# Spreading both halves of a key tile in one VectorE operation, loading a weight in two parts, and a new instruction order, in a four-layer attention kernel

## The chip, the cores and the metric

The kernel runs on one core of a Trainium2 chip, as one launch. The metric is the device time in microseconds; the median of three runs of the kernel before is 464.93 us (463.89 to 466.02). The profile is of one execution, with a span of 462.5 us from the first to the last instruction.

The engines are called as the profile calls them: PE is TensorE (matrix multiplication; PEld is its weight load), DVE is VectorE, ACT is ScalarE, POOL is GpSimd and SP is SyncE, which here issues only transfers. Both SP and ACT issue transfers ("SPq" and "ACTq" in the profile).

## The reference

Four layers are applied to x, 2048 rows of 512 numbers, with residual additions. Layers 1 and 3 are sliding-window attention with weights A; layers 2 and 4 are linear attention with weights B. There are 32 heads of 16 numbers each.

```python
def _A_ref(x, wqkv, wo):            # window of 256 keys
    qkv = (x @ wqkv) ...            # q, k, v by head
    scores = einsum("bhqd,bhkd->bhqk", q, k) * (Dh ** -0.5)
    mask = (i - j >= 0) & (i - j < W)
    p = softmax(where(mask, scores, -1e9))
    return einsum("bhqk,bhkd->bhqd", p, v) ... @ wo

def _B_ref(x, wqkv, wo):            # linear attention
    phi = lambda t: where(t > 0, t + 1, exp(t)) + 1e-6
    pq, pk = phi(q), phi(k)
    kv = einsum("bhsd,bhse->bhde", pk, v);  z = sum of pk over s
    o = einsum("bhqd,bhde->bhqe", pq, kv) / (pq . z + 1e-6)
    return o ... @ wo

x = x + _A_ref(layernorm(x), A_wqkv, A_wo)
x = x + _B_ref(layernorm(x), B_wqkv, B_wo)
x = x + _A_ref(layernorm(x), A_wqkv, A_wo)
x = x + _B_ref(layernorm(x), B_wqkv, B_wo)
```

## The kernel before

The rows are treated in four blocks I of 512. Every piece of work is recorded as an operation with the engines that may do it, and a fixed list, `ORDER`, says in which order the 2582 operations are emitted and on which engine each runs (18H is operation 18, a transfer; P is PE, A is ACT, V is DVE, G is POOL, S is SP). A small model of the engines, the planner, walks through this list. It does not choose the order; it chooses which bank of PSUM (the accumulator memory of PE, eight banks) each operation takes, and puts filler matmuls (`fill`) where it expects PE to stand idle.

```python
def is_warm(t):                      # does the planner expect PE at full clock at time t?
    k = int(t / self.WIN)
    for w in range(max(warm, default=-1) + 1, k + 1):
        warm[w] = mac.get(w - 1, 0) >= self.FULL
    return warm[k]
...
if start - free["PE"] > self.GAP:    # an expected gap of PE: fill it with matmuls of the identity
    ...
    fill = (b[0], m) if m else fill
...
def fill(k, n):
    for _ in range(n):
        nc.tensor.matmul(psb[:, k, :], lhsT=identb[:], rhs=..., start=True, stop=True)      # line 491
```

The keys. A projection writes 128 rows (8 heads) by 512 keys to one bank of PSUM. The scores need every key twice, once with the rows of the other head of a pair set to zero. So the result is multiplied by `eo`, a pair of 0/1 columns, and each key becomes two neighbouring columns. Five buffers of 256 keys each (`NH = 5`) are used in rotation; `half(8*I)` and `half(8*I+4)` are the two of block I: 0 and 1, 2 and 3, 4 and 0, 1 and 2.

```python
NH, NPT = 5, 5
kbd = [fp.tile([P, NCT, 4, 64, 2], BF, name=f"kbd{k}") for k in range(NH)]

def k_unit(key, I, t):
    o, s, ps = proj(... wA columns of k, tile t ..., reads=[B("wA", 1, min(t, 1))], ...)   # 4 matmuls, line 569
    for hf in range(2):
        r = half(8 * I + 4 * hf)
        def fe(e, hf=hf, r=r):
            if e == "ACT":
                for h in range(2):
                    nc.scalar.mul(kbd[r][:, t, :, :, h], ps()[:, hf*256:(hf+1)*256]..., eo[:, h:h+1])   # line 777
                return
            nc.vector.tensor_tensor(kbd[r][:, t, :, :, :]..., ps()[:, hf*256:(hf+1)*256]...,
                                    eo[:]..., op=ALU.mult)                                              # line 779
        pl.op({"DVE": .68, "ACT": .9}, fe, reads=[B("eo")], deps=[o], writes=[B("k", r, t)], use=[s])
```

The rest of an attention block: `scores` multiplies queries with these keys (line 822), ACT takes the exponential (line 840), DVE or POOL zeroes what is outside the window (lines 868 and 873), and `pv_group` multiplies with the values (line 901). The values get from a staging tile to their place by transfers on SP (`vbd<-vst`, line 798). The normalised rows reach PE transposed, as `xnT`, by a transposing transfer on SP (line 579) or by PE itself (line 588); layernorm writes them to `xn` (line 701 on DVE), and a buffer of `xn` is free again once its transpose has read it.

The weights. Five parts of `wA` and the first rows of x are loaded at once. The other loads are issued by ACT where the order puts them; the time given first is the earliest at which the planner lets one start:

```python
for b, t, c, fn in ((b_x[8:NT], 15.0, 3.0, lambda e: load_x(nc.scalar, 8, NT - 8)),
                    ([B("woA")], 25.0, 1.5, lambda e: nc.scalar.dma_start(woA[:], wcols(A_wo, 0))),
                    ([B("wB")], 40.0, 4.5, lambda e: nc.scalar.dma_start(wB[:], wcols(B_wqkv, 0, 3))),
                    ([B("woB")], 70.0, 1.5, ...)):
    o = pl.op({"ACT": .5}, fn, after=t)
    pl.op({"HBM": c + 2.0}, lambda e: None, deps=[o], writes=b)
```

`wB` is the weight of the linear layers, read by `bk_unit` and `bv_unit` (columns 512 to 1535, keys and values) and by `bq_units` (columns 0 to 511, queries).

Of the kernel before, what the change touches and what calls it, by code (L numbers as in the profile page):

```python
# [9 lines left out]
ALU = mybir.AluOpType  # L10
F32 = mybir.dt.float32
BF = mybir.dt.bfloat16
# [138 lines left out]
class Planner:  # L151
# [25 lines left out]
    def run(self):  # L177
# [7 lines left out]
        def is_warm(t):  # L185
            k = int(t / self.WIN)
            for w in range(max(warm, default=-1) + 1, k + 1):
                warm[w] = mac.get(w - 1, 0) >= self.FULL
            return warm[k]
# [50 lines left out]
18H 17H 36V 6G 19H 20H 12A 41V 46V 37G 38V 51A 14A 23H 2G 42G 15A 13A 21H 3G 47G 10V 22H 24H 43V 39P 40V 25H 44P  # L240
52V 48V 45V 75P 76V 49P 53P 54V 77S 78P 50V 26H 65P 55P 79V 60P 62A 63P 16V 57V 56V 67A 0G 58P 80S 314V 59V 66V
64V 61A 27A 329V 73P 87P 88A 81P 4G 9G 1G 91P 84P 28H 82A 83S 5G 70P 315G 316V 319V 330G 324V 89G 96P 72V 71V
92A 7G 320G 101P 74A 85A 325G 95G 102A 321V 90G 68P 69V 317P 97A 107P 322P 86S 104G 94G 98G 106G 103G 108A 109G
115P 105G 99G 116A 331V 318V 354P 93G 332P 119P 323V 617V 618G 8G 100G 120A 110G 124P 117G 355V 326V 357P 125A
333V 629V 625V 621V 123G 129P 356S 327P 111P 112P 113P 128G 630G 130A 131G 358A 133V 328V 122V 135P 143P 114V
136A 121V 127G 619V 126G 134V 360P 144A 132G 147P 137G 118G 138G 631V 361V 359S 337P 620S 148A 916V 152P 139P
140P 153A 157P 928V 622G 141P 626G 158A 142V 149G 146G 160G 162G 155V 156G 363P 150G 161G 338A 364V 163P 171P
627V 623V 154V 164A 166G 165G 334P 347P 632S 362S 917G 159G 151G 175P 348V 172A 145V 336V 342P 343V 173G 920V
335V 180P 176A 185P 653P 181A 167P 168P 169P 174V 654V 186A 29A 921G 624S 628S 191P 199P 177G 183G 179V 918V
365S 192A 646P 170V 636P 647V 187V 190V 929G 184G 182G 203P 188G 189G 178V 200A 656P 208P 204A 194G 31A 213P  # L250
657V 193V 637V 201G 195P 641P 214A 196P 217V 206G 197P 209A 215V 930V 219P 227P 220A 642V 352P 216V 228A 198V
212G 211G 205G 218G 221G 924V 202G 207G 233P 210V 651P 652V 234A 366P 222G 232G 223P 224P 225P 371P 237V 655S
229G 230G 658S 235V 236G 238G 367A 372A 353V 231G 375P 376A 925G 239P 662P 373G 931S 379G 380P 226V 240V 659P
919S 374G 370G 663V 926V 381A 660V 369G 386P 339P 340V 341V 378V 387A 922V 377G 390P 391A 384V 344P 346V 398P
242S 345V 385G 633P 382G 635V 399A 248S 403P 349P 383G 251S 368G 389G 407P 245S 388G 393V 400V 634V 394P 392G
401V 923S 927S 404A 408A 402G 412P 395P 396P 418P 351V 413A 419A 416V 414V 935P 422P 423A 415V 405V 664S 417G
409G 410G 406V 350V 430P 397V 431A 936V 638P 421G 435P 436A 411V 420V 424V 643P 439P 426P 645V 440A 425G 444P
427P 445A 428P 450P 451A 644V 454P 639V 648P 446G 449G 437G 640V 438V 432V 452G 434V 455A 448G 661S 429V 433V
462P 940P 467P 453V 463A 443G 457G 468A 442G 447G 456V 932P 471P 941V 441G 458P 649V 241V 472A 459P 476P 477A
465G 460P 482P 650V 933V 934V 937P 483A 469V 464V 486P 243P 494P 487A 495A 474V 475V 461V 470V 244V 466G 479G  # L260
480G 945P 499P 500A 484V 481G 473V 488V 478G 489V 485G 490P 497V 939V 946V 938V 503P 504A 491P 508P 492P 514P
254V 505G 509A 510G 512G 493V 507G 515A 511V 249P 518P 519A 246P 32H 250V 516V 498G 526P 502G 527A 33A 517G 255G
247V 506G 513G 520G 532G 252P 521V 942P 536P 665P 501V 253V 496V 522P 530G 535G 523P 524P 944V 528G 537A 534G
533G 541V 540V 666A 531G 538G 529V 539V 670P 542P 674P 671A 675A 525V 543V 262V 551S 545S 548S 554S 952P 679P
680A 673V 685P 258V 943V 678V 953V 955P 672V 263G 677G 668G 686A 667G 256G 681V 956V 689P 688G 687G 690A 683G
684G 682G 257S 950P 669V 697P 698A 546P 702P 552P 692V 676V 547V 703A 706P 691G 693P 707A 711P 694P 557V 553V
565V 712A 699V 264G 695P 717P 270P 705G 259G 718A 951V 721P 729P 555P 271A 696V 549P 957S 722A 713G 558G 709V
720G 715V 704V 559V 266V 700V 730A 714G 710G 716G 719G 734P 735A 556V 701G 708G 723G 738P 724V 550V 569V 725P
743P 265S 954S 739A 260V 744A 731G 261S 267G 566G 726P 727P 749P 750A 732V 742G 958P 747G 570G 753P 754A 728V
272V 959V 544V 274P 761P 766P 762A 275V 741V 755V 746V 273V 767A 961P 571G 751V 756G 737G 745G 740G 733G 276P  # L270
770P 775P 962V 768V 752G 736G 284P 748V 757P 758P 759P 277A 776A 769V 771A 561V 278V 777V 781P 285A 780G 782A
279V 773V 760V 778V 785P 786A 560S 280P 793P 794A 764V 763G 774G 288P 798P 799A 572S 286V 287V 765G 562G 779G
567V 947P 802P 784G 772G 803A 783V 289V 789P 807P 563G 788G 787V 790P 808A 810G 949V 801V 805G 795V 568S 564S
948V 281V 791P 811G 804G 960S 813P 814A 815G 282P 605P 606A 268V 792V 797V 817P 818A 796V 806G 825P 601P 602A
283V 816V 826A 819G 812V 607V 963S 800G 613P 614A 809G 835P 608V 832G 827G 820G 833G 836A 603V 604V 609P 830V
831V 615V 964P 610A 965A 829G 828V 821P 822P 823P 969P 834V 616V 839G 840G 837G 838V 824V 841P 842V 970A 269S
290P 291A 973P 974A 978P 979A 844S 967G 971G 847S 850S 611V 981G 294P 612V 573P 295V 984P 985A 292V 293V 968V
966G 980G 845P 988P 989A 848P 982V 983G 996P 997A 846V 976V 972G 1001P 849V 991G 1002A 574A 853S 990G 975V 860V
986G 987G 977G 851P 852V 577P 1005P 1006A 992P 861G 1010P 1011A 864V 578V 856V 575V 576V 993P 994P 1016P 1017A
998G 296P 857G 1020P 995V 1015V 1021A 1012G 1013V 854P 1014V 1028P 1029A 297V 579P 580A 1033P 1034A 1008G 587P  # L280
1007G 1018G 1037P 1038A 1009G 1019V 11V 1004V 999G 1000G 1003G 1023V 855V 1022V 1031V 858G 1024P 1025P 1026P
1042P 1043A 1048P 1049A 1044G 1030G 865G 581V 582V 1027V 868V 1039G 862G 583P 1052P 588A 1053A 1041V 584V 591P
1060P 1061A 592V 593P 585P 859S 1032G 35S 589V 590V 586V 1065P 1066A 863S 1035V 1046V 1040V 1047G 594A 1045G
1050G 1055V 597P 876P 1069P 1070A 598V 1036G 843V 1051G 1074P 1075A 1056P 1064G 1054G 866G 1057P 877V 1077G
1068V 867S 1058P 1067G 1080P 1081A 595V 1072V 882P 596V 1084P 1085A 599P 1079V 883V 1092P 1063G 1073G 1059V 872P
1076V 600V 1078G 890P 1093A 1071G 1097P 891V 873A 1098A 298P 299A 1101P 1102A 874V 1106P 878P 1082G 875V 1107A
1083V 1062V 869G 1087G 1086V 300V 1095V 1088P 1089P 879A 1090P 1112P 1113A 870G 871S 1110G 1100G 1104G 1099V
1116P 1117A 301V 886P 1091V 1105G 880V 1111G 1103G 302P 881V 1096V 884P 1109G 1108V 1115V 887A 303A 1124P 1134P
1114G 1094G 885V 1119G 1118G 888V 304V 889V 305V 1120P 1121P 1122P 1135A 1123V 1125A 34H 1133V 1132V 1131V 892P
1139G 1136G 893A 894V 1129V 1138G 895V 896P 1137G 1128G 1127G 306P 1126G 897A 1130G 1140P 898P 1141V 1143P 899V  # L290
1142V 307A 1144A 1151P 308G 1152V 1147P 1148A 1155P 1145P 1149P 309V 900P 1153P 1146V 1156A 1157P 1150V 1237V
1159A 1160A 1161G 1164V 1154V 1165A 310P 901A 1158V 1169A 1162P 1163V 1174A 1238P 1239V 904P 902V 1166G 1170G
311A 1167P 903V 1179P 312V 1171G 313V 1175G 1183P 1168A 905A 1172P 1189P 906V 1173A 1176G 907V 1185P 1193P 1180A
1184A 1186A 1181V 1190V 1182V 1177P 1178V 1194A 1187V 1188V 1195G 1197P 908P 1207P 1198V 1196V 1208A 1191P 1199P
1200A 1203P 1209V 1192V 1210V 1201V 1202V 909A 1215P 1204A 1216A 1217V 1218V 1211P 1205P 1206V 1223V 912P 913A
1225V 1219P 1240P 1241P 1224G 910V 1220A 1212A 914V 915V 1242A 1226G 911V 1213V 1227P 1214V 1243A 1221G 1228A
1222V 1244V 1851P 1538P 1539V 1233P 1536P 1235P 1537V 1234A 1231P 1236A 1247P 1248V 1232A 1229P 1852P 30H 1245P
1230A 1540P 1246V 1853A 1541V 1546P 1249P 1250V 1854A 1251P 1252V 1253P 1254V 1544P 1548A 1545V 1855V 1255P
1542P 1549G 1257A 1258G 1262A 1259G 1267A 1263A 1256V 1547V 1264G 1260P 1268A 1261A 1543V 1856P 1272A 1265P
# [76 lines left out]
def build(ctx, tc, A_x, A_wqkv, A_wo, B_x, B_wqkv, B_wo, out, force_safe=False):  # L376
# [95 lines left out]
    def fast_network(ctx_f):  # L472
# [52 lines left out]
        def B(*key):  # L525
            return bufs.setdefault(key, Buf())
        def half(m):
            return (m // 4) % NH
# [913 lines left out]
```

## Time and profile before

| | busy us | share of the span | instructions |
|---|---|---|---|
| PE | 436.0 | 94% | 6035 |
| DVE | 367.7 | 79% | 969 |
| ACT | 379.1 | 82% | 442 |
| POOL | 259.6 | 56% | 737 |

The page lists, for each engine, the busy time; then the span in 40 slices with one digit of busy share for each; then the chain of work that ended last. The groups of instructions follow, by line and shape: how many, their busy time together, the mean of one, and what ended the idle time of the engine before them. In a timeline, the first column is the start and the second the duration of a merged run of instructions; square brackets hold the idle time of that engine before it and what ended it. Matmuls overlap one another, so that the listed duration of one is longer than the distance from one to the next.

### The profile page before, as it was taken

The page shows a single profiled execution, that of the slowest core. Times are in us where ns is not written, and L with a number is a line of the kernel's source. Part 1 is how long each engine was busy: PE and PEld are TensorE (multiplying, and loading weights), DVE is VectorE, ACT ScalarE, POOL GpSimd, SP SyncE. Part 2 cuts the span into 40 slices and gives each one's busy share as a digit, 9 for nine tenths or more (in the row PEclk, how much of TensorE's full clock was granted, in tenths as well). Part 3 has the DMA queues.
Part 4 walks back from the last instruction along what each step waited for, and adds up shares of the span by engine and source line. Part 5 has one row for each costly group of instructions (what it writes and reads, how often), then busy time and mean ns, then how long its engine had stood idle before and what let it go on. Part 6 is the DMA issues. An engine that isn't in the chain of part 4 may idle for free.

```text
span 462.5 us, 15167 instructions
## 1 busy us (share of the span) xinstructions
PE 436.0 (94%) x6035; PEld 227.6 (49%) x6103; DVE 367.7 (79%) x969; ACT 379.1 (82%) x442; POOL 259.6 (56%) x737
## 2 busy tenths in 40 slices
PE   6997999999999999999999998999999989999893
PEld 2454454555555556543445454555455545464331
DVE  5996687878887987878887888888887786777883
ACT  7798599989999999655888888989999989967630
POOL 5298354367755575532325586855685549455432
PEclk8999899999999999999999999999999999999998
DMA  7424631023222010000021124111322122100014
GB/s 227 122 45 119 171 81 28 1 72 71 38 48 60 13 26 15 2 1 0 4 46 26 28 44 73 40 36 26 71 53 45 23 28 27 23 2 1 1 45 144
DMA packets 53806, 22.29 MB, mean 48 GB/s; under 512 B 38368, under 2 KB 53216, under 8 KB 53728
## 3 DMA queue, kind: packets, MB, share of 16 engines
q1 hardware_dynamic: 49760, 16.80, 17.2%
q10 hardware_dynamic: 3968, 4.46, 3.0%
q8 instruction: 49, 0.80, 0.7%
q14 instruction: 29, 0.24, 0.2%
HBM read 6.29 MB, written 2.10 MB: 18 GB/s over the span
## 4 chain that ended last, share of the span: by engine, by line
PE 75%; ACT 8%; issue 5%; DVE 5%; DMA 4%; POOL 2%; SPq 1%; ACTq 0%; DVEq 0%; POOLq 0%
PE psb L569 40%; PE psb L901 16%; PE psb L822 14%; ACT pt L840 7%; DMA wA<-in_A_wqkv_dram 2%; PE psb L1117 1%; PE psb L588 1%; DMA vbd<-vst 1%; DMA oT<-o_sb 1%; SPq L798 1%; POOL pqT L978 1%; PE psb L491 1%; PE psb L1091 1%; POOL pt L873 1%; DVE pqT L981 1%
## 5 line engine op out<-in xcount | busy, mean ns | idle before, releaser
L840 ACT ACTIVATE pt<-psb 128x1536 bf16<-128x1536 f32 (+2 forms) x246 | 284.1, 1215 | 30.8 <-PE psb L822 19.8
L873 POOL TENSOR_SCALAR_AFFINE_SELECT pt<-pt 128x192 bf16<-128x192 bf16 (+2 forms) x535 | 158.3, 330 | 112.0 <-ACT pt L840 107.9
L822 PE MATMUL psb<-qT,kbd 32*128 32x320 bf16 (+4 forms) x1440 | 94.0, 254 | 4.0 <-ACT pt L840 2.8
L901 PEld LDWEIGHTS <-pt 128*128 128x128 bf16 x2880 | 77.9, 96 | 13.6 <-issue 9.8
L901 PE MATMUL psb<-vbd,pt 128*128 128x34 bf16 x2880 | 83.7, 178 | 0.2 <-DVE xres L755 0.2
L868 DVE TENSOR_TENSOR pt<-pt,tri 128x128 bf16<-128x128 bf16 (+4 forms) x262 | 63.5, 275 | 12.1 <-ACT pt L840 11.8
L822 PEld LDWEIGHTS <-kbd 32*128 32x128 bf16 x1440 | 40.2, 92 | 66.3 <-issue 59.9
L569 PE MATMUL psb<-xnT,wA 128*128 128x512 bf16 x241 | 63.8, 387 | 3.6 <-issue 2.8
L569 PE MATMUL psb<-wB,xnT 128*128 128x512 bf16 x235 | 61.6, 380 | 1.6 <-DVE pqT L978 0.4
L569 PEld LDWEIGHTS <-xnT 128*128 128x128 bf16 x384 | 32.6, 98 | 42.5 <-issue 12.8
L779 DVE TENSOR_TENSOR kbd<-psb,eo 128x512 bf16<-128x512 f32 x58 | 37.8, 679 | 2.9 <-PE psb L569 2.6
L569 PEld LDWEIGHTS <-wA 128*128 128x128 bf16 x256 | 21.9, 99 | 30.1 <-issue 10.4
L569 PE MATMUL psb<-wA,xnT 128*128 128x512 bf16 x116 | 33.2, 392 | 2.7 <-DMA wA<-in_A_wqkv_dram 1.9
L569 PE MATMUL psb<-woA,oT 128*128 128x512 bf16 x120 | 31.5, 381 | 3.1 <-DMA oT<-o_sb 1.3
L569 PE MATMUL psb<-xnT,wB 128*128 128x512 bf16 x121 | 31.5, 380 | 0.9 <-DVE vflags L968 0.5
L569 PE MATMUL psb<-wkv,pqT 128*128 128x512 bf16 x123 | 29.6, 380 | 0.3
L690 DVE BATCH_NORM_STATS2 ln_st<-xres 128x6 f32<-128x512 f32 (+1 forms) x39 | 26.5, 680 | 1.7 <-DMA xres<-in_A_x_dram 1.6
L916 DVE TENSOR_TENSOR o_sb<-psb,rall 128x384 bf16<-128x384 f32 (+1 forms) x48 | 24.6, 513 | 1.7
L975 ACT ACTIVATE pqT<-psb 128x512 bf16<-128x512 f32 x32 | 18.9, 599 | 8.2 <-PE psb L569 6.4
L556 DVE CAST qT<-psb 128x512 bf16<-128x512 f32 x29 | 19.8, 685 | 6.9 <-PE psb L569 6.3
L624 POOL TENSOR_TENSOR ln_rs<-ln_rs,mhalf 128x1 f32<-128x1 f32 x39 | 21.9, 562 | 3.2
L981 DVE SCALAR_TENSOR_TENSOR pqT<-psb,pqT 128x512 bf16<-128x512 f32 x32 | 21.8, 687 | 1.6 <-POOL pqT L978 1.0
(122 smaller groups left out, 485.9 us busy)
## 6 DMA issues: line engine op xcount, KB each, us to landing
vbd<-vst SPq DMA_DIRECT2D x128, 34.0 KB, 1.9
out_dram<-ost SPq DMA_DIRECT2D x16, 128.0 KB, 1.8
wB<-in_B_wqkv_dram ACTq DMA_DIRECT2D x1, 1536.0 KB, 7.9
xres<-in_A_x_dram ACTq DMA_DIRECT2D x1, 1024.0 KB, 5.5
xnT<-xn SPq DMA_TRANSPOSE x40, 2.5
wA<-in_A_wqkv_dram SPq DMA_DIRECT2D x1, 512.0 KB, 7.1
xres<-in_A_x_dram SPq DMA_DIRECT2D x1, 512.0 KB, 8.1
woA<-in_A_wo_dram ACTq DMA_DIRECT2D x1, 512.0 KB, 5.7
```

Source lines behind the costliest of these rows:

```text
L556: (nc.scalar.copy if e == "ACT" else nc.vector.tensor_copy)(dst(), src())
L569: nc.tensor.matmul(t["t"][:], lhsT=lhs(c), rhs=rhs(c), start=(c == 0), stop=(c == NCT - 1))
L624: nc.gpsimd.tensor_tensor(out, out, mhalf[:, 0:1], op=ALU.pow)
L690: nc.vector.bn_stats(t["st"][:], x())
L779: nc.vector.tensor_tensor(kbd[r][:, t, :, :, :].rearrange("p m k h -> p (m k) h"), ps()[:, hf * 256:(hf + 1) * 256].unsqueeze(2).to_broadc ...
L822: nc.tensor.matmul(A[:, x, at[x]:at[x] + w, :], lhsT=kbd[half(m)][32 * rg:32 * rg + 32, tt, m % 4, :, :], rhs=qT[I % 2][32 * rg:32 * rg + ...
L840: nc.scalar.activation(body[:, x:y, 0:pos[x], :], t["A"][:, x:y, 0:pos[x], :], ACT.Exp, scale=0.25)
L868: nc.vector.tensor_tensor(v, v, mt, op=ALU.mult)
L873: nc.gpsimd.affine_select(out=v, in_=v, compare_op=ALU.is_ge, fill=0.0, base=1 if kind == 0 else -2, pattern=[[0, n], [2 * sg, 64]], chann ...
L901: nc.tensor.matmul(t["O"][:, u, g, :, :], lhsT=PT[:, s0:s0 + 2, :], rhs=vbd[half(m)][:, m % 4, :, grp[g], :], start=(n == 0), stop=(n == l ...
L916: nc.vector.tensor_tensor(o_sb[:, u0:u0 + nu, h0 * DH:(h0 + 2 * ng) * DH].rearrange("p u (h e) -> p u h e", e=DH), Ov[:, :, :, 0:DH], r.to ...
L981: nc.vector.scalar_tensor_tensor(out=dst(), in0=ps()[:], scalar=1.0 + 1e-6, in1=dst(), op0=ALU.add, op1=ALU.max)
```

## The change

It has five parts. The first takes the two halves of a key tile together: the five buffers become one tile, so that two neighbours lie side by side, and where the two of a block are neighbours (blocks 0, 1 and 3; not block 2, which has 4 and 0), one VectorE operation spreads all 512 keys. In these blocks ACT can no longer do it.

```diff
-        kbd = [fp.tile([P, NCT, 4, 64, 2], BF, name=f"kbd{k}") for k in range(NH)]
+        kall = fp.tile([P, NH, NCT, 4, 64, 2], BF, name="kall")
+        kbd = [kall[:, k] for k in range(NH)]
...
+            r0 = half(8 * I)
+            if r0 + 1 < NH:
+                def fe(e):
+                    nc.vector.tensor_tensor(kall[:, r0:r0 + 2, t, :, :, :].rearrange("p r m k h -> p r (m k) h"),
+                                            ps().rearrange("p (r c) -> p r c", r=2).unsqueeze(3).to_broadcast([P, 2, 256, 2]),
+                                            eo[:].unsqueeze(1).unsqueeze(1).to_broadcast([P, 2, 256, 2]), op=ALU.mult)
+                pl.op({"DVE": 1.2}, fe, reads=[B("eo")], deps=[o], writes=[B("k", r0 + hf, t) for hf in range(2)], use=[s])
+                return
             for hf in range(2):
```

The second loads `wB` in two parts, keys and values first, and lets these loads come earlier in the planner's time; the readers name the part that they need:

```diff
-                            reads=[B("wB"), B("xq", i)], ...          # bk_unit, bv_unit
+                            reads=[B("wB", 1), B("xq", i)], ...
-                                    reads=[B("wB")] + ...             # bq_units
+                                    reads=[B("wB", 0)] + ...
-                            ([B("woA")], 25.0, 1.5, lambda e: nc.scalar.dma_start(woA[:], wcols(A_wo, 0))),
-                            ([B("wB")], 40.0, 4.5, lambda e: nc.scalar.dma_start(wB[:], wcols(B_wqkv, 0, 3))),
+                            ([B("woA")], 19.0, 1.5, lambda e: nc.scalar.dma_start(woA[:], wcols(A_wo, 0))),
+                            ([B("wB", 1)], 22.0, 3.0, lambda e: nc.scalar.dma_start(wB[:, :, D:3 * D], wcols(B_wqkv, 1, 2))),
+                            ([B("wB", 0)], 27.0, 1.5, lambda e: nc.scalar.dma_start(wB[:, :, 0:D], wcols(B_wqkv, 0))),
```

The third moves the times at which the planner expects the first transfers to land. The fourth makes it assume a full PE clock from 25 us on:

```diff
+            if t > 25.0:
+                return True
...
-        ... ([B("wA", 2)], 8.0), ([B("wA", 1, 1)], 10.0), ([B("wA", 0, 1)], 9.5), (b_x[4:8], 12.0)]
+        ... ([B("wA", 2)], 9.5), ([B("wA", 1, 1)], 11.0), ([B("wA", 0, 1)], 10.5), (b_x[4:8], 12.5)]
```

The fifth is a new `ORDER` for all operations, 2560 of them now (cut):

```diff
-18H 17H 36V 6G 19H 20H 12A 41V 46V 37G 38V 51A 14A 23H 2G 42G 15A 13A 21H 3G 47G 10V 22H 24H 43V 39P 40V 25H 44P
-... (131 more lines)
+18H 17H 19H 0G 20H 38V 48V 39G 49G 15A 43V 44G 2G 53A 10V 40V 50V 23H 45V 54V 46P 6G 25H 24H 21H 1G 47V 41P 26H
+... (130 more lines)
```

What it is for: fewer operations on the engine that empties PSUM, each of which has a fixed cost; weights that are there before they are needed; and an order that fits the changed costs.

## The prediction

> **What bounds the kernel now.** I read four views: the page (busy shares, slices, chain), the groups by shape, the timeline of two stretches, and the busy time in stretches of 10 us. The page first.
>
> ```profile
> PE 436.0 (94%) x6035; PEld 227.6 (49%) x6103; DVE 367.7 (79%) x969; ACT 379.1 (82%) x442; POOL 259.6 (56%) x737
> PE   6997999999999999999999998999999989999893
> ACT  7798599989999999655888888989999989967630
> PEclk8999899999999999999999999999999999999998
> PE 75%; ACT 8%; issue 5%; DVE 5%; DMA 4%; POOL 2%; SPq 1%; ACTq 0%; DVEq 0%; POOLq 0%
> ```
>
> PE is the bound nearly everywhere: 75% of the chain that ended last, 9 tenths in most slices. In the attention blocks ACT is close behind it; from 50 to 180 us the stretches show PE busy 9.2 to 9.95 of 10 us and ACT 8.3 to 9.7. DVE, which the change relieves, is at 79% and has 5% of the chain. So time can come only from what makes PE idle or slow: 26 us of the span have no matmul at all. In the stretches these are 3.7 us before 10 us, 7.6 us after the last matmul, 2.8 us in 40 to 50, and about 1.4 us each in 280 to 290 and 370 to 380. The slice with PE 7 and the ACT 5 in the same place is the largest inner one. The timeline there:
>
> ```profile
> 38.76 2.52 SPq L579 DMA_TRANSPOSE xnT<-xn  x2
> ...
> 40.78 0.38 ACTq L1136 DMA_DIRECT2D woA<-in_A_wo_dram  x1
> ...
> 46.16 3.28 PE L569 MATMUL psb<-xnT,wA 128*128 128x512 bf16 x7 [2.67 <-issue]
> 46.16 0.41 DVE L701 TENSOR_SCALAR xn<-xres,ln_mv,ln_rs 128x512 bf16<-128x512 bf16 x1 [2.78 <-POOL pt L873]
> ```
>
> PE stops for 2.67 us and DVE for 2.78 us and both start again at 46.16. The names of the releasers mislead: in the built program both wait for the transposes xnT<-xn issued at 38.76. Their median is 2.5 us to landing; these took about 6, because the load of woA (0.5 MB, 5.7 us to landing by the page) was issued at 40.78 in the middle of them. Then PE is slow: 7 matmuls take 3.28 us, where a long run elsewhere in the chain has 33 in 7.23 us, 0.22 each. ACT next starts an exponential only at 50.02, after 4.37 us idle. The stop cost 2.67 + (3.28 - 7 x 0.22 = 1.7) = 4.4 us.
>
> The start, from the same view:
>
> ```profile
> 8.06 5.80 ACT L550 COPY vbd<-zero 128x2176 bf16<-128x2176 bf16 x3
> 9.28 1.86 PE L569 MATMUL psb<-wA,xnT 128*128 128x512 bf16 x4 [1.90 <-DMA wA<-in_A_wqkv_dram]
> ...
> 14.23 1.87 DVE L548 MEMSET vbd<- 128x2176 bf16 x1 [0.40 <-DVE vst L556]
> ...
> 16.02 1.22 DVE L779 TENSOR_TENSOR kbd<-psb,eo 128x512 bf16<-128x512 f32 x2
> 16.14 2.10 ACT L777 ACTIVATE kbd<-psb,eo 128x256 bf16<-128x256 f32 x5
> ...
> 19.13 1.45 ACT L840 ACTIVATE pt<-psb 128x1536 bf16<-128x1536 f32 x1 [0.89 <-PE psb L822]
> ```
>
> The first weights land at 9.28 and the first exponential starts at 19.13. Between them DVE clears a buffer for 1.87 us before it spreads keys, and ACT spends 15.73 to 18.24 on six key halves' columns.
>
> **What the Trainium skill says.** "VectorE: DVE Perf Modes", section "The TRN2 errata", says that an operation pays a fixed extra latency whatever its size, so that larger operations pay it less often. The groups agree for one operation alone:
>
> ```profile
> L779 DVE TENSOR_TENSOR kbd<-psb,eo 128x512 bf16<-128x512 f32 x58 | 37.8, 679 | 2.9 <-PE psb L569 2.6
> L1121 DVE TENSOR_TENSOR pqT<-pqT,psb 128x1024 bf16<-128x1024 bf16 x16 | 19.1, 1216 | 3.4 <-PE psb L1117 3.1
> L777 ACT ACTIVATE kbd<-psb,eo 128x256 bf16<-128x256 f32 x12 | 5.0, 549 | 1.9 <-PE psb L569 1.9
> ```
>
> Twice 679 is 1358, one of double size is 1216. But two back to back take 1.22 us together in the start above: the next begins before the first has ended, and the saving is gone. "DMA: Bandwidth & Descriptors", section "Issuing engines are not separate DMA queues", says that transfers issued by different engines run on the same 16 DMA engines; the slowed transposes beside woA agree. "TensorE: Matmul & The Clock Gate", Part 1, says that an idle PE falls to half clock and needs some 3.4 us of work to come back; the seven slow matmuls (0.43 us apart in the same timeline) agree. "Perfetto Trace Analysis", section "Identifying the Most-Contended Engine", warns that matmul busy time doesn't tell the headroom of PE; I therefore count gaps and pace, not the 94%.
>
> **The change part by part.**
>
> 1. Merged spreading. Of 64 halves, 58 were on DVE and 6 on ACT (12 instructions). Now 48 halves are 24 merged operations and 16 stay single on DVE, none on ACT. DVE: 24 x 1.216 - 42 x 0.679 = 29.2 - 28.5 = +0.7 us. ACT: -12 x 0.549 = -6.6 us. So the part named first saves VectorE nothing in total; it takes work off ACT. On the path it is worth little, because kbd stands in front of PE for almost no time (no wait of PE names it); half of ACT's 12 instructions are at the start, half at 190 to 238 us, where ACT is less loaded (5 to 8 us of 10). I count 0 here and leave the start to part 3.
> 2. The new order moves other operations between engines. Counting instructions of each shape in both built orders and multiplying by the mean of the groups: ACT -5.6 us in all (three value evacuations come to it, at 0.60), DVE -0.8, POOL +1.6. PE has the same matmuls except 4 fillers fewer (37 to 33); after the start 25 fillers become 15. A filler marks idleness that the planner knows of: 10 x 0.22 = 2.2 us less. Changes between scores and other matmuls fall from 390 to 380, worth under 1 us. I count -1.5.
> 3. Start. The six column operations leave ACT (2.5 us between 15.73 and 18.24), DVE clears its buffer before the first keys instead of after two value tiles, and two query evacuations go to ACT. In the new order ACT has three buffer clears (2.0 each), one xnT (0.6), two values and two queries (0.6 each) after 8.1 us: 8.1 + 6 + 5 x 0.6 = 17.1, against 19.13. DVE gives: clear until 11.4, a merged operation 1.2, two statistics of 0.87 after x at about 12, a merged 1.2, so keys at about 16, scores, first exponential at about 17. I count -1.8.
> 4. Loads. woA is now issued after the 21st exponential, behind the point where PE needs the transposes, and the two parts of wB after the 12th and the 17th. Three transposes follow the first part, and the second may meet their end. But between those transposes and PE's need of them there are now about 7 exponentials of 1.2 us, about 8 us, against 4 before. So most of the 4.4 us should go; the 1 MB load can eat a part. I count -3.5. wB itself gives nothing by being early: its first reader starts at 110 us, and it was issued at 50.05 with 7.9 us to landing.
> 5. New close waits. Taking PE's work between the issue of a transpose and PE's wait for it (0.222 us a projection matmul, 0.045 a score, 0.0265 a value product, from the chain), the old order has none of xnT under 4.2 us; the new has one of 2.9 at about three quarters of the program, and more at 4.2 to 4.6 in the second half. The oT transposes are as close as before (2.7 to 4.5). A transpose needs about 1.2 us of SP and 2.5 to land: I count +1.8.
>
> Sum: -1.5 - 1.8 - 3.5 + 1.8 = -5.0 us, so 464.9 - 5.0 = 459.9.
>
> **The rivals.** (a) The search only exchanges the stalls: what I found at 43 us I know because I have its trace, and the new order has such places that I can't see. For it: the planner puts no contention into its transfers, so it can't have removed that stall by intent. Then about 0 to -1: 464. (b) The wB load of 1 MB meets the transposes as woA did and PE stops at 33 to 40 us instead, with its clock falling again; then part 4 is lost: 463.4. For it: the load comes directly ahead of three transposes; against it: the 8 us. (c) The merged operation makes the waits longer: 1.2 us before either half is ready, and a bank held as long, on a DVE that is at 79%. For it: PSUM banks are few; against it: pairs took 1.22 anyway. It would add 1 to 3 us: 462. (d) ACT and not PE sets the pace of the attention blocks; then the 5.6 us taken off ACT count in full, and it is 455.
>
> **Range and chances.** The gains rest on two places that the trace shows; the losses on an unseen order. I take 4.5 us as the spread, with a little more room above: 454 to 465.5. Faster by over 2% means under 455.6: this needs (d) on top of the sum, 0.16. Slower by over 2% means over 474.2: 0.02. Within: 0.82.
>
> **What would show it.** Right: the first exponential at about 17 us; no stop of PE over 1 us between 35 and 50 us, and no matmuls at 0.43 us there; merged operations of about 1.21 us, 24 of them, in a DVE total that differs by under 3 us; ACT busy about 5 us less. Wrong: a stop of PE with the wB load in flight (b); PE waiting for the merged operation (c); idle PE beside oT or xnT transposes after 280 us that adds over 3 us (a). A time under 454 or over 466 would mean that the order's effect in the middle of the blocks, which I took as 1.5 us, was mis-sized.

## The result, and the profile after

The changed kernel takes 458.43 us (median of 4 runs, 456.40 to 459.87) against 464.41 us (463.66 to 466.02) for the kernel before beside it: a ratio of 0.9864, 95% interval 0.9816 to 0.9911. The prediction was 459.9 us, so its sum was right; most of its terms were not.

The page of the changed kernel, with the same lines as before: busy time, two rows of slices, the granted clock, and the engines' shares of the chain that ended last.

```profile
PE 433.0 (95%) x6036; PEld 225.8 (49%) x6099; DVE 365.8 (80%) x949; ACT 375.0 (82%) x433; POOL 262.3 (57%) x742
...
PE   7897999999999999999999998999999999999995
...
ACT  7888499998999999775777988998999989977731
...
PEclk9999799999999999999999999999999999999999
...
PE 77%; ACT 6%; DVE 6%; DMA 5%; issue 3%; POOL 1%; SPq 1%; ACTq 0%; DVEq 0%
```

The reader is to look at the fifth slice (45.7 to 57.1 us). ACT has 4 there, the clock 7. The largest inner stop of the kernel before, which part 4 of the prediction expected to lose, is still there. Its timeline in the changed kernel (start, duration, instruction, and in brackets the idle time before it and what ended it):

```profile
32.15 0.37 ACTq L1147 DMA_DIRECT2D wB<-in_B_wqkv_dram  x1
...
37.85 5.18 SPq L581 DMA_TRANSPOSE xnT<-xn  x3
...
39.66 0.44 ACTq L1148 DMA_DIRECT2D wB<-in_B_wqkv_dram  x1
...
43.72 0.40 ACTq L1146 DMA_DIRECT2D woA<-in_A_wo_dram  x1
...
46.15 1.87 PE L571 MATMUL psb<-xnT,wA 128*128 128x512 bf16 x4 [2.48 <-DMA xnT<-xn]
...
48.60 0.92 ACT L850 ACTIVATE pt<-psb 128x896 bf16<-128x896 f32 x1 [3.44 <-PE psb L832]
```

woA no longer meets the transposes, but wB does. Its first part is in flight from 32.15 to 37.65, and the single transpose issued at 33.81 takes 4.8 us to landing. Its second part, of 0.5 MB, is in flight from 39.66 to 44.85, and the last two of the three transposes, issued at 39.13 and 40.44, take 6.1 and 5.6 us. PE stands 2.48 us, then runs 4 matmuls in 1.87 us (0.47 each), and ACT stands 3.44 us. The start did change:

```profile
9.92 1.87 DVE L550 MEMSET vbd<- 128x2176 bf16 x1 [0.40 <-DVE xnT L593]
11.71 1.16 DVE L777 TENSOR_TENSOR kall<-psb,eo 128x1024 bf16<-128x1024 f32 x1
...
14.40 1.19 DVE L777 TENSOR_TENSOR kall<-psb,eo 128x1024 bf16<-128x1024 f32 x1
...
16.27 2.26 ACT L850 ACTIVATE pt<-psb 128x1536 bf16<-128x1536 f32 x2
...
21.01 0.69 DVE L558 CAST vst<-psb 128x512 bf16<-128x512 f32 x1 [2.69 <-DMA vbd<-vst]
```

The first exponential starts at 16.27 instead of 19.13, but VectorE then waits 2.69 us for value spreading transfers, and 1.6 of the 2.9 us are gone by the fifth exponential.

A profile's busy shares don't tell where two versions drift apart. For that I list the start of the k-th exponential in each trace: 246 of them, on the path in the attention blocks, so they are mileposts. The first row is us, the others are differences from the kernel before, and the last column is the profiled span. (The orders differ a little in which exponential is the k-th; differences under 1 us at one post mean little. A row is one execution; that of old_then_new took 466.59 us, 2.7 more than its median.)

```
k-th exponential    1     5    21    29    37    45    85   117   181   245   end
before           19.1  24.9  44.2  59.0  68.9  78.8 130.0 175.2 315.8 405.3 462.5
after            -2.9  -1.3  -0.5  +0.7  +0.2  +0.6  +1.0  +0.2  -1.8  -2.3  -6.0
old_order        -1.9  +2.3  +2.2  +4.4  +4.5  +4.7  +4.7  +4.7  +4.8  +4.7  +4.6
new_then_old     -2.7  -1.3  -1.2  -3.5  -3.9  -3.5  -3.2  -3.6  -4.2  -4.4  -5.8
old_then_new     -1.1  +3.1  +3.0  +5.2  +5.3  +5.5  +5.5  +5.5  +4.5  +3.7  +2.3
new_old_tail     -2.8  -0.9  -0.6  -0.1  -0.6  -0.2  +0.2  -0.6  -2.7  -3.6  -4.4
split_dve        -2.0  -0.4  -0.2  +0.1  -0.4  -0.0  +0.4  -0.3  -2.2  -2.2  -4.8
old_merge_vv     -0.4  -0.4  -0.1  -2.9  -2.8  -2.8  -2.8  -2.8  -3.1  -2.8  -2.5
old_merge_all    +3.4  +6.0  +6.1  +5.3  +5.4  +5.4  +5.4  +5.4  +5.5  +7.2  +7.5
old_merge_start  +4.3  +7.0  +7.0  +9.1  +9.1  +9.1  +9.1  +9.1  +9.5  +9.4  +8.0
late_loads       -2.6  -1.3  -1.5  -4.0  -4.4  +0.5  +1.4  +0.8  -1.9  -3.1  -4.7
late_loads_2     -2.1  -1.4  -1.5  -4.4  -4.8  -4.4  -4.0  -4.8  -6.8  -7.4  -8.8
late_loads_x     -2.1  -2.0  -1.3  -4.6  -5.0  -4.4  -3.9  -4.7  -6.8  -7.6  -9.7
before_late      -0.3  -0.3  -0.3  -2.8  -2.8  -2.8  -2.8  -2.8  -2.5  -2.1  -1.5
```

The row "after": 2.9 us won at the start are back to nothing at the 37th exponential; nothing happens up to the 117th; 2.5 us are won between it and the 245th, and 3.7 in what follows. The gain lies in the last 280 us, where the prediction had counted -1.5 for the order and +1.8 against it. The other rows are the experiments.

### The profile page after: what moved, and what is told of

The parts are those of the page before. It is cut to its first block, busy times and chain, and to the rows that moved or that the text cites. A ratio compares the mean times of both kernels' runs of the same rounds, so it can differ in the third digit from the quotient of the medians.

```text
span 456.5 us, 15164 instructions
## 1 busy us (share of the span) xinstructions
PE 433.0 (95%) x6036; PEld 225.8 (49%) x6099; DVE 365.8 (80%) x949; ACT 375.0 (82%) x433; POOL 262.3 (57%) x742
## 4 chain that ended last, share of the span: by engine, by line
PE 77%; ACT 6%; DVE 6%; DMA 5%; issue 3%; POOL 1%; SPq 1%; ACTq 0%; DVEq 0%
PE psb L571 43%; PE psb L911 15%; PE psb L832 14%; ACT pt L850 5%; DMA wA<-in_A_wqkv_dram 2%; PE psb L1127 1%; DMA xnT<-xn 1%; PE psb L590 1%; DMA vbd<-vst 1%; DMA oT<-o_sb 1%; PE psb L1101 1%; PE psb L1032 1%; SPq L808 1%; DMA xres<-in_A_x_dram 1%; POOL pt L883 1%
## 5 line engine op out<-in xcount | busy, mean ns | idle before, releaser
L832 PE MATMUL psb<-qT,kall 32*128 32x320 bf16 (+4 forms) x1440 | 93.2, 254 | 1.9 <-ACT pt L850 1.1
L832 PEld LDWEIGHTS <-kall 32*128 32x128 bf16 x1440 | 39.5, 92 | 63.4 <-issue 56.4
L571 PE MATMUL psb<-xnT,wA 128*128 128x512 bf16 x239 | 65.0, 389 | 4.5 <-DMA xnT<-xn 2.5
L777 DVE TENSOR_TENSOR kall<-psb,eo 128x1024 bf16<-128x1024 f32 x24 | 28.9, 1210 | 2.1 <-PE psb L571 1.9
L925 DVE RECIPROCAL rall<-psb 128x24 f32<-128x24 f32 (+1 forms) x48 | 13.8, 287 | 17.7 <-PE psb L911 16.8
L985 ACT ACTIVATE pks<-psb 128x512 bf16<-128x512 f32 x32 | 19.2, 607 | 5.7 <-PE psb L571 5.7
```

The costliest lines, as they stand in the source:

```text
L571: nc.tensor.matmul(t["t"][:], lhsT=lhs(c), rhs=rhs(c), start=(c == 0), stop=(c == NCT - 1))
L777: nc.vector.tensor_tensor(kall[:, r0:r0 + 2, t, :, :, :].rearrange("p r m k h -> p r (m k) h"), ps().rearrange("p (r c) -> p r c", r=2).un ...
L832: nc.tensor.matmul(A[:, x, at[x]:at[x] + w, :], lhsT=kbd[half(m)][32 * rg:32 * rg + 32, tt, m % 4, :, :], rhs=qT[I % 2][32 * rg:32 * rg + ...
L925: nc.vector.reciprocal(r, Ov[:, :, :, DH:VW])
L985: nc.scalar.activation(dst(), ps()[:], ACT.Exp)
```

## The experiments

The theory after the first comparison (O): the new order makes the gain, mostly late; merging is worth nothing by itself. The rivals: merging with its relief of ScalarE makes it, or the start and the loads do, as the prediction said. Every experiment was run next to the kernel before; its ratio is to those runs. The experiments were not all on one chip, so medians of different ones compare less surely than their ratios.

### Which part of the change, and where

Both orders contain the same operations, so the old order can be written with the changed kernel's numbers. In these four kernels the PSUM bank and the filling matmuls of each operation are taken from the kernel whose order it follows, so that nothing else moves. At 1284 operations (226 us by the plan) and at 2362 (407 us) both orders have done exactly the same set, and the one can be continued by the other. Ratios leave out runs over 1.5% above the fastest of their kernel, which here are 30 of the 51 runs of the kernel before (456.41 to 466.56 us, median 463.55), so that these four ratios lie 0.003 to 0.006 above those of the medians given.

```diff
-ORDER = NEW
+ORDER = OLD                          # old_order: a merged pair stands where its first half stood
+ORDER = NEW[:1284] + OLD[1284:]      # new_then_old
+ORDER = OLD[:1284] + NEW[1284:]      # old_then_new
+ORDER = NEW[:2362] + OLD[2362:]      # new_old_tail
```

old_order. 

> The changed kernel with the order, the PSUM banks and the filling matmuls of the kernel before; only the merged spreading (24 operations of 1.21 us, each at the place of the first half of its pair) and wB's two parts, issued next to each other at 44 us, are left of the change. Theory O (the new order makes the whole gain): 464.4, within 1.3 of the kernel before. Rival M (merging and its 6.6 us less on ScalarE carry it): 459 to 461. Rival (c) of the prediction (the longer operation lengthens waits): 465.5 to 467.5.

Measured: 469.19 us, ratio 1.0167 (1.0106 to 1.0228). Merging and parts in the old order don't gain and don't break even: they cost 5.6 us against 463.55. None of the theories had it; rival (c) comes nearest. The mileposts say where: +4.4 us by the 29th exponential, and then 4.4 to 4.8 to the end, through 19 more merged operations.

new_then_old. 

> The changed kernel with the new order up to 226 us of the plan (the place where both orders have done the same 1284 operations), then the old order to the end. Theory O2 (the gain arises late: the two traces stand only 0.7 us apart at 229 us): 463.7 (462.5 to 464.8). Rival, the prediction's own sum (parts 3 and 4, the start and the loads, lie before this place: -1.8 and -3.5, and -0.7 of part 2): 458.4 to 459.5.

Measured: 461.55, ratio 1.0013 (0.9975 to 1.0052). This lies between the two theories: the median is 2.0 us under that of the kernel before, and the interval of the ratio holds 1.

old_then_new. 

> The changed kernel with the old order up to 226 us of the plan and the new one from there on; the counterpart of the run before. Theory O2: 459.1 (458 to 460.3), so that this and its counterpart add up to the whole gain of 6.0. Rival, the prediction's own sum: 464 to 465.5.

Measured: 463.90, ratio 1.0036 (0.9999 to 1.0073). This is about the time of the kernel before. Theory O2, which is O with the gain put late, was wrong with its 459.1; the rival's number is near, but not for its reason, as follows.

The two halves can't be added from the kernel before, since merging in the old order starts 5.6 us behind it. Against old_order both halves of the new order gain: 469.2 - 461.6 = 7.6 us for the first, 469.2 - 463.9 = 5.3 for the second. So O doesn't hold as it was put, since the early half gains as much as the late one. The first half of the new order pays for the merging, the second half is what is left over.

new_old_tail. 

> The changed kernel with the new order up to 407 us of the plan (2362 operations) and the old order for the last 47 us. Theory O2, by the traces' distance of 3.5 us at 400 us, 2.5 more being won in the tail (the old tail has a chain of GpSimd steps of 8.7 us at 428 to 438 us): 460.9. Rival (the whole gain lies in the tail): 463.5 or more. Rival (the tail brings nothing by itself, it only hands on what was won before): 458.4.

Measured: 460.02, ratio 0.9958 (0.9922 to 0.9994). The estimate of 460.9 was near; the new tail is worth 1.6 us by the medians, 2.5 by the distance of each from its own runs of the kernel before (6.0 and 3.5 us), where single runs spread from 456.17 to 463.12. The chain of the kernel before in the tail (start, duration, what):

```profile
428.55 1.35 POOL kvn L1066 x2
...
429.98 1.92 POOL pqT L978
431.90 3.48 issue
...
435.43 1.93 POOL pqT L978
```

and of the changed kernel:

```profile
427.78 1.95 POOL pqT L988
...
432.03 1.14 DVE pqT L1131
...
433.21 1.02 PE psb L1127 x4
```

Before, GpSimd's pieces and an issue make 8.7 us of the chain; the new order leaves one such piece, 1.95 us, with VectorE's and TensorE's work behind it.

### What merging costs

split_dve writes each merged operation as two, at the same place of the new order.

```diff
-nc.vector.tensor_tensor(kall[:, r0:r0 + 2, t, ...], ps() as [P, 2, 256, 2], eo, op=ALU.mult)
+for hf in range(2):
+    nc.vector.tensor_tensor(kbd[r0 + hf][:, t, ...], half hf of ps() as [P, 256, 2], eo, op=ALU.mult)
```

> The changed kernel where each merged operation is written as two VectorE operations of 512 keys one after the other, at the same place of the same order. Prediction part 1 (the merged one costs as much as the pair back to back): 458.4, within 1. Rival (two operations pay a fixed cost twice, 24 x 0.15 us, a third of it on the path): 459.5 to 460.5. Rival (c) (the longer operation lengthens waits, since the first half is there only with the second): 456 to 457.

Measured: 458.41, ratio 0.9870 (0.9827 to 0.9914), where the changed kernel has 0.9864. The groups of the changed kernel (busy us, mean ns):

```profile
L777 DVE TENSOR_TENSOR kall<-psb,eo 128x1024 bf16<-128x1024 f32 x24 | 28.9, 1210 | 2.1 <-PE psb L571 1.9 <-ACT xn L642 0.2
...
L789 DVE TENSOR_TENSOR kall<-psb,eo 128x512 bf16<-128x512 f32 x16 | 10.7, 683 | 0.2 <-PE psb L571 0.2
```

and of the split one:

```profile
L778 DVE TENSOR_TENSOR kall<-psb,eo 128x512 bf16<-128x512 f32 x48 | 30.4, 678 | 2.1 <-PE psb L571 1.9 <-ACT xn L642 0.2
```

48 x 678 would be 32.5 us, but the busy time is 30.4, since pairs overlap; merging saves VectorE 1.5 us of busy time in all and the kernel nothing that can be measured (the interval is 2 us to either side). Part 1 of the prediction holds.

The next two take the kernel before, with its order and its banks, and merge some or all pairs at the place of the first half; the second half is not written.

```diff
-def fe(e, hf=hf, r=r):
+def fe(e, hf=hf, r=r, n=number of this operation):
+    if n in HOW:                         # old_merge_vv: the 20 pairs with both halves on VectorE
+        if HOW[n] == "first":            # old_merge_all: all 24
+            (the merged operation)       # old_merge_start: 2, with halves on ScalarE, before the first exponential
+        return
```

old_merge_vv. 

> The kernel before, order and banks untouched, with only those 20 pairs merged whose halves both ran on VectorE; the 4 pairs with a half or two on ScalarE (two of them before the first exponential) stay split, and wB comes in one part. Theory A (the old order with all merged lost 4.7 us in the first 60 us because two halves that ScalarE took beside VectorE at the start now queue on VectorE): 463.6, as before. Rival (c) (merging lengthens waits anywhere): 466 to 468.5. Rival (wB's two parts did it): 463.6 too, told apart by the next run.

Measured: 462.14, ratio 0.9971 (0.9940 to 1.0002). This is the time of the kernel before: 20 merged operations at the old places cost nothing that shows.

old_merge_all. 

> The kernel before, order and banks untouched, with all 24 pairs merged, wB still in one part. Theory A: 467 to 469.5, nearly all of the 5.6 us that the old order with merging and parts lost. Rival (wB's two parts did it): 463.6, as before.

Measured: 470.07, ratio 1.0134 (1.0091 to 1.0178). Four pairs make the difference of 7.9 us between these two. wB is in one part here, and the time is that of old_order, so the two parts of wB are not what cost.

old_merge_start. 

> The kernel before with only two pairs merged, the two with halves on ScalarE before the first exponential (the tiles that the 45th to 58th place of the order spread). Theory A (the whole loss of merging in the old order is made by these two, as the traces stand 6.0 us apart from the 5th exponential on): 468.5 to 470. Rival (it is the sum of many longer waits): 463.5 to 465.

Measured: 471.44, ratio 1.0168 (1.0120 to 1.0217). Two merged operations cost all of it, 7.9 us. Why 2 x 1.2 us can cost that much is in the timeline of this run:

```profile
15.60 1.23 DVE L778 TENSOR_TENSOR kall<-psb,eo 128x1024 bf16<-128x1024 f32 x1 [1.94 <-PE psb L569]
17.22 1.87 DVE L548 MEMSET vbd<- 128x2176 bf16 x1 [0.40 <-issue]
19.01 1.22 DVE L786 TENSOR_TENSOR kall<-psb,eo 128x512 bf16<-128x512 f32 x2
20.15 1.22 DVE L778 TENSOR_TENSOR kall<-psb,eo 128x1024 bf16<-128x1024 f32 x1
...
20.29 1.02 PE L569 MATMUL psb<-xnT,wA 128*128 128x512 bf16 x4 [3.00 <-DVE kall L786]
...
22.81 0.61 PE L829 MATMUL psb<-qT,kall 32*128 32x192 bf16 x6 [1.50 <-DVE qT L556]
...
23.46 1.45 ACT L847 ACTIVATE pt<-psb 128x1536 bf16<-128x1536 f32 x1 [9.61 <-PE psb L829]
```

Compare the lines of the kernel before in the prediction. There ScalarE took these halves while VectorE cleared its buffer at 14.23. Now the merged operation stands in VectorE's queue at that place, in front of the clearing; its projection isn't there, the queue waits 1.94 us in order, and the clearing starts at 17.22, 3.0 us late. The next key halves follow 3.0 us late (16.02 to 19.01), TensorE waits 3.00 and 1.50 us, ScalarE stands idle for 9.61 us, and the first exponential is at 23.46, 4.3 us late. PE's clock then falls: the slices of 20 to 25 and 25 to 30 us have 0.73 and 0.59 of full speed, and the distance grows to 7.0. ScalarE, with nothing in front of it, also issues the last load of x at 7.96 us instead of 15.80. That isn't what delays the start: TensorE's instructions up to 13 us begin within 0.2 us of those of the kernel before. In the new order the clearing comes first (9.92) and no merged operation before 17 us waits. The merged operation isn't slow; it is a matter of where it stands in the queue of an engine that works in order.

### The stop at 40 to 50 us

late_loads issues the weights where no transpose is in the queue.

```diff
-29A after exponential 21, 31A after 12, 33A after 17, 35A after 43     # woA, wB part 1, wB part 0, woB
+29A after exponential 37, 31A after 44, 33A after 50, 35A after 54
```

> The changed kernel with woA, wB's two parts and woB issued after the 37th, 44th, 50th and 54th exponential (some 62, 74, 84 and 92 us) instead of the 21st, 12th, 17th and 43rd; between the 37th and the 61st no transposing transfer and no value spreading transfer is in the queue, and each weight lands before its first reader. Theory S (loads that meet the xnT transposes make the stop at 40 to 46 us and the cold stretch behind it; the traces of two runs with and without the cold stretch stand 3.2 us apart): 455.2 (454 to 456.5), the transposes at 33 to 43 us back at 2.5 us, no matmul of 0.43 us between 40 and 55 us. Rival (the transposes are late whoever loads, or TensorE would have run out of work there anyway): 458 to 459.

Measured: 459.53, ratio 0.9899 (0.9859 to 0.9939): nothing gained. By the mileposts it is both theories in turn: at the 37th exponential 4.4 us ahead of the kernel before, at the 45th 0.5 behind. Its timeline at that place:

```profile
67.06 5.34 SPq L808 DMA_DIRECT2D vbd<-vst  x8
...
68.92 0.38 ACTq L1146 DMA_DIRECT2D woA<-in_A_wo_dram  x1
69.42 4.62 ACT L850 ACTIVATE pt<-psb 128x1536 bf16<-128x1536 f32 x4 [3.94 <-DMA vbd<-vst]
```

A transfer's issue can wait, and with it everything behind it on its engine. In the built program woA's issue waits for a semaphore that a value spreading transfer, eight transfers earlier in the program, still held: SyncE was behind its place in the order, that transfer was issued only at 67.06, and ScalarE stood 3.94 us. (The planner added three filling matmuls of its own in this kernel; the next one has the banks and fillings of the changed kernel.)

late_loads_2 moves only woA on, by five exponentials.

```diff
-29A after exponential 37
+29A after exponential 42
```

> As the run with late loads, with woA after the 42nd exponential instead of the 37th; nothing else differs from the changed kernel. Theory S: in the first try the stop at 40 to 55 us was gone (4.4 us ahead of the kernel before at the 37th exponential, where the changed kernel is 0.2 behind), but 4.9 us were lost between the 37th and the 45th, where ScalarE stood 3.9 us in front of woA's issue, which waits for a value spreading transfer; issued later it waits for nothing: 453.8 (452.5 to 455). Rival (PE has slack there, the gain is lost again in later waits): 457.5 to 458.5.

Measured: 455.52 (453.07 to 455.94), ratio 0.9808 (0.9766 to 0.9850). S holds in the trace, 4.8 us ahead at the 37th exponential and 4.4 at the 45th, where the changed kernel was 0.2 and 0.6 behind. In the medians it gains less on the changed kernel, 2.9 us, or 2.1 by the distance of each from its own runs of the kernel before (8.1 and 6.0). Transposes and stop in this run:

```profile
37.01 5.06 SPq L581 DMA_TRANSPOSE xnT<-xn  x3
...
43.87 1.02 PE L571 MATMUL psb<-xnT,wA 128*128 128x512 bf16 x4 [1.24 <-DMA xnT<-xn]
```

The second and third of the three transposes land 4.3 and 4.0 us after their issue instead of 6.1 and 5.6, the single one ahead of them 2.6 instead of 4.8. The stop is 1.24 us instead of 2.48, and the four matmuls behind it take 1.02 instead of 1.87. Expected was that the transposes go back to 2.5; these two didn't. A part of that wait is not the loads'.

late_loads_x also halves x's last load.

```diff
-27A: load_x(nc.scalar, 8, 8)
+27A: load_x(nc.scalar, 8, 4); after exponential 7: load_x(nc.scalar, 12, 4)
```

> As the run before, and x's last 1 MB in two parts of 512 KB, the second issued after the 7th exponential (some 27 us) instead of at 15 us with the first. Theory X (the 1 MB load slows the value spreading transfers at 16 to 21 us, for which VectorE then waits 2.7 us and TensorE 1.7 us): 1.0 to 1.7 below the run before, 452.5. Rival (a wait elsewhere takes its place, or the second part meets the next transfers): the same as the run before.

Measured: 454.46 (454.00 to 455.04), ratio 0.9800 (0.9762 to 0.9838); not to be told from the run before. In the trace it is 0.6 us ahead of it at the fifth exponential, and 0.2 behind at the 21st. What took it back, in its timeline:

```profile
24.30 0.41 ACTq L406 DMA_DIRECT2D xres<-in_A_x_dram  x1
...
28.55 0.89 PE L911 MATMUL psb<-vbd,pt 128*128 128x34 bf16 x29 [0.83 <-DMA vbd<-vst]
```

The second part meets the next value spreading transfers: the rival. The wait only moved.

before_late does the same to the kernel before.

```diff
-woA after exponential 19, wB after 22, woB after 58
+woA after exponential 42, wB after 45, woB after 54
```

> The kernel before with woA, wB (one part) and woB issued after the 42nd, 45th and 54th exponential; banks, filling matmuls and order of all else untouched. Theory S: the stop at 43 to 50 us goes, which the prediction's part 4 put at 4.4 us: 459.1 to 460. Rival (the stop is not made by the loads): 463 to 464.

Measured: 461.98, ratio 0.9969 (0.9947 to 0.9991): a gain of 1.6 us, between the two. In the profiled run PE still stops:

```profile
44.97 1.89 PE L570 MATMUL psb<-xnT,wA 128*128 128x512 bf16 x8 [1.80 <-issue]
```

so the 4.4 us that the prediction read there were not all the loads': the old order by itself leaves a stop of 1.80 us, and the last transpose takes 4.5 us to landing without a load, where it took 6.0 with woA. Nor is the stop the same in every execution: in old_merge_vv, with woA still at its old place, it was 1.42 us, and at the 37th exponential both traces are 2.8 us ahead.

### Why so short a difference of stops makes 3 to 5 us

Two traces of the same instructions disagree. new_then_old and the changed kernel have the same order up to 226 us; at the 29th exponential the one is 3.5 us ahead of the kernel before, the other 0.7 behind. Here is 45 to 50 us in the changed kernel (busy us and instructions of PE, weight load, DVE, ACT and POOL; then the granted clock, the DMA share and GB/s):

```profile
45.00:50.00 5.00, 3.85 (x12) 1.15 (x13) 1.06 (x4) 1.08 (x2) 0.87 (x4) 0.51 0.38 122
```

and in new_then_old:

```profile
45.00:50.00 5.00, 5.00 (x65) 2.44 (x64) 3.10 (x8) 2.98 (x4) 0.68 (x3) 1.00 0.33 108
```

65 matmuls against 12, at a clock of 1.00 against 0.51. The stop itself was 1.75 against 2.48 us. The longest stop of PE between 40 and 58 us in all traces, in order of length, with the lowest granted clock of the slices of 5 us from 45 to 60 us, and the time in us that the clock record of the trace stands at half there:

```
late_loads_x     none over 1   1.00   0        before           2.67   0.66   3.4
late_loads_2     1.24          1.00   0        split_dve        2.64   0.83   3.4
old_merge_vv     1.42          1.00   0        new_old_tail     2.83   0.76   3.4
late_loads       1.52          1.00   0        old_order        3.78   0.50   6.8
new_then_old     1.75          1.00   0        old_merge_start  3.83   0.52   6.8
before_late      1.80          1.00   0        old_then_new     3.87   0.50   6.8
old_merge_all    1.89          0.68   3.4
after            2.48          0.51   6.8
```

At this place every stop up to 1.80 us left the clock alone, and every one from 1.89 us on lost it. So the cost of a stop has a step. Its height, from the pair above: 4.2 us lie between them at the 29th exponential, 0.7 already at the 21st, and the stops differ by 0.73; 2.8 us remain for the slow stretch. An estimate agrees: at half clock for 6.8 us, TensorE does at most 3.4 us less work; for 3.4 us, 1.7.

The length of a stop alone doesn't decide, as two other places show. late_loads_x stops longer at the start and keeps the full clock:

```profile
8.92 1.07 PE L590 MATMUL psb<-identb,xn 128*128 128x128 bf16 x16 [2.45 <-DVE xn L703]
5.00:10.00 5.00, 2.55 (x24) 1.50 (x23) 4.54 (x13) 4.94 (x10) 3.39 (x12) 1.00 1.03 337
10.00:15.00 5.00, 5.00 (x24) 2.20 (x23) 4.56 (x7) 4.88 (x6) 0.00 (x0) 1.00 0.12 40
```

and old_merge_all loses it late, for 3.4 us, after a shorter one:

```profile
379.35 1.84 PE L569 MATMUL psb<-woA,oT 128*128 128x512 bf16 x4 [1.56 <-DMA oT<-o_sb]
380.00:385.00 5.00, 5.00 (x97) 2.98 (x96) 2.48 (x6) 2.76 (x3) 1.41 (x4) 0.71 0.01 2
```

What else decides stays open. The Trainium skill, "TensorE: Matmul & The Clock Gate", Part 1, gives an idle window of about 3.4 us after which the clock falls; here it also fell after stops of 1.56 to 2.83 us, and the measurement decides.

The clock also goes with the spread of one kernel's runs. Of the 94 runs of the kernel before beside the experiments, the 22 with a mean granted clock of 0.989 or less have a median of 465.3 us, the 20 with 0.994 or more one of 461.2. And it goes with the loads: the mean granted clock is 0.995 to 0.998 in all 12 runs of late_loads_2 and late_loads_x, but reaches 0.995 in only 13 of the 45 of the changed kernel, split_dve, new_old_tail and new_then_old, which have the same order in the first half with the loads at the changed kernel's places. (late_loads has 0.990 to 0.995: in its trace the 3.94 us of ScalarE stop PE too, for 3.17 us, and the clock is at half for 3.4 us from 72.4 us on. In the old order the loads do less: 6 of 22 runs of before_late reach 0.995, 10 of the 94.) That the stop at 45 us is what makes the clock differ between runs of one kernel is argued; only one run of each was traced.

## Why the prediction was right, point by point

The time was right and the range held it, but three of five terms were mis-sized, and they cancelled. That the sum came out within 1.5 us is luck: what the order gained late stood in for what the loads didn't.

Part 1 (merging: 0). Right for the kernel as changed: 24 operations of 1210 ns against the 1216 taken, VectorE's total 1.9 us less, and split_dve takes the same time. (The section on the TRN2 errata that the prediction names speaks of operations that read SBUF; these read their keys from PSUM, and the measured durations are what counts.) ScalarE is busy 4.1 us less, where 5.6 was counted in parts 1 and 2 together. What the part didn't see is that it isn't independent of the order: at the old places two of the 24 cost 7.9 us.

Part 2 (the new order elsewhere: -1.5). Too small. From the 117th exponential to the end the changed kernel gains 6.2 us on the kernel before, and the other five traces that run the new order to the end 3.2 to 5.5; the medians give the second half of the order 5.3. Only the tail could be tied to a named wait (GpSimd's pieces, 1.6 to 2.5 us). Between 175 and 405 us it is 1.8 to 3.9 us in the seven traces that run the new order there, in many small pieces; which of them, no run here settles.

Part 3 (start: -1.8). The first exponential came at 16.27 us; 17 was predicted. In the traces with the new start it is 2.0 to 2.9 us early. But at the fifth it is 0.4 to 2.0: what the prediction's working left out is VectorE's wait for the value spreading transfers, 2.69 us in the changed kernel.

Part 4 (loads: -3.5). Wrong, and this is the step that failed: "between those transposes and PE's need of them there are now about 7 exponentials of 1.2 us, about 8 us". The trace has the last of the three transposes leave at 40.44, and PE needs it at 46.15 - 2.48 = 43.67: 3.2 us. The transposes stand behind value spreading transfers in SyncE's queue, so counting exponentials from their place in the order counts from a time at which they haven't left. The mechanism itself, a load that slows the transposes and a clock that falls, is borne out. The last transpose ahead of the stop takes 4.8 to 6.4 us in the ten traces with a load in flight and 4.0 to 4.5 in the four without, and the mean clock is 0.995 or more in all 12 runs of late_loads_2 and late_loads_x. But it was taken too large: of the 6.0 us in the kernel before, 4.5 are there without woA. And the 5.0 us by which the milepost moves from the changed kernel to late_loads_2 aren't the loads' worth, since new_then_old, with the loads unmoved, stands 4.1 us ahead of the changed kernel there; in the times it is 2.1 to 2.9 us.

Part 5 (close waits: +1.8). Nothing of it came. PE's waits in the changed kernel (total us, times, longest):

```profile
PE psb L571 <- DMA xnT<-xn: 2.5, 1, 2.5
PE psb L571 <- DVE vst L558: 2.1, 2, 1.7
...
PE psb L571 <- DMA oT<-o_sb: 0.8, 1, 0.8
```

One wait for xnT, and it is the stop at 46 us; oT has 0.8 where it had 1.3.

The rivals. (a) is half true: the stop of 2.67 us with its cold stretch was exchanged for one of 2.48. (b) is true in part: wB's load makes the stop, but it is the 0.5 MB part, and at 43.67 us instead of 33 to 40. Its time of 463.4 was wrong, because part 2 brought 1.7 to 4.7 us more than counted. (c) is false in the new order (split_dve), and in the old one for the 20 pairs of old_merge_vv; the 7.9 us of the other pairs come from the place in the queue and not from a longer operation. (d), that ScalarE sets the pace, was not tried by itself; the chain gives ACT 6%, where it had 8%.

The version that beats both: late_loads_x, or late_loads_2 within the error, at 0.980 of the kernel before (454.46 us against 463.58). The changed kernel has 0.9864 and its interval overlaps theirs a little; the mileposts show the difference of 5 us at the place where the edit acts.

## What to carry to other kernels

Where operations are placed by hand or by a search, a merged operation is to be judged together with a new order: at the old place it can stand ahead of its input and hold up an engine that works in order. Keep large loads out of the stretch in which transposes are waited for, and put their issue where the earlier transfer that holds their semaphore has surely landed, or the issuing engine stands. When two runs or two versions differ by 3 to 5 us and the profile shows stops that differ by 1, look at the granted clock behind the stop before looking for more causes.

## What the runs showed of the hardware

In all 14 traces the granted clock of TensorE is either full or half. Between 40 and 58 us, stops of 1.24 to 1.80 us left it full (five traces), and stops of 1.89 to 3.87 us were followed by 3.4 or 6.8 us at half (four traces each). Elsewhere a stop of 2.45 us left it full and one of 1.56 us didn't. A transpose by DMA whose usual time to landing is 2.4 to 2.6 us took 4.7 to 5.2 beside a load of 1 MB (the single one at 33 us, four traces; 2.6 in three without the load). The last one ahead of the stop took 4.8 to 6.4 beside a load of 0.5 MB, and 4.0 to 4.5 with no load about. Two VectorE operations of 512 columns one after the other take 1.22 us together, as one of 1024 does (1.21): joining them saves instructions and hardly any time.
